# Attention, MoE and a second MoE on one core: who makes the swapped copy of v, and when in its step

## The chip, the cores and the metric

The kernel runs on one core of one Trainium2 chip. The metric is the time of one execution on the device in microseconds (us), taken as the median of several runs. The core has five engines that work through their own queues of instructions in order: PE (matmuls; the loading of its weights is listed as PEld), DVE, ACT (ScalarE), POOL (GpSimd) and SP, which here only issues loads. POOL also issues DMAs, and in the profile such a DMA takes POOL's own time while it is issued. A semaphore wait holds everything behind it in the same queue.

## The reference, cut to what matters

```python
def _attn_ref(q, k, v):                       # (8, 8, 576, 64) each, float32
    scores = scale * matmul(q_c, k_c^T)       # chunks of 64 tokens, each with itself
    attn = softmax(scores)
    out = matmul(attn, v_c)

x = attn_out as (4608 tokens, 512)
x = _moe_ref(x)      # tokens with x @ w_skip > 0 go through one of 8 experts, the argmax of x @ w_gate
return _moe2_ref(x)  # max(x@w1, x@w2, x@w3), relu, @ w_out
```

The change concerns the product `matmul(attn, v_c)` of the first line alone.

## The kernel before

The program has three phases. Phase 1 is the attention and the routing, in 36 steps `t` of 128 tokens; phase 2 runs the experts, phase 3 the second MoE. In phase 1 a step holds two chunks of 64 tokens for each of 8 heads. The tokens of a chunk lie in 64 of the 128 partitions, and a matmul of 64 rows takes weights and data from the same half. So for half of the (chunk, head) pairs the values `v` are wanted in the other half: `cross(t)` (L219 to L225) makes `vm[t]`, a copy of `v_all[t % 8]` with its halves swapped, in two copies of 64 x 260 floats, one for each half. DVE makes them for t = 0 and 1, POOL from t = 2 on. Four `vm` tiles exist at a time. The matmuls of `values(t)` (L301) read `v_all`, `vm` and the transposed exponentials `aT`.

In loop step t the code is written as follows, and for t below 34 the order on DVE, ACT and POOL is that of the code, and PE's is that of the code throughout the phase: rank of an earlier group of tiles; `send_id(t-9)`; loads of q and k; `cross(t)`; `pair_heads` (L231, on POOL: the copies `qr` and `kr`, two steps ahead of their use); `values(t-2)`; `scaled(t-2)` on DVE; the load of v for step t+6; `scores(t)` (L260) on PE and `shift(t)` (L269, L271) on DVE; `exp_transpose(t-1)` (L285 on PE, its copy `aT`, L288, on ACT); the transposes of q and k with copies `qT` and `kT` (L247, ACT); the gate's logits of tile t-3 (L344 on PE, copy `lg`, L349, on ACT); `exponentials(t)` (L278, ACT); the transpose of x of tile t-2 (L333 on PE) with the copy `xt` in `x_out` (L338, ACT); and then the routing of a group of four tiles in some of the steps (`route`, L360 to L389, on DVE; the rank matmuls L416 and L417 on PE), with the store of the group's rows (`store_x`, L492, issued by POOL). In eight of the steps a piece of the experts' weights is split too (L93 on ACT, L94 on DVE or POOL).

`send_id(t)` (L470) is an indirect DMA, issued by POOL: it scatters the 128 token numbers of a tile to the slots that the routing has given them in `ids_dram`. It is done from loop step 9 on, one in most steps, and stands directly ahead of `cross` on POOL's queue. Phase 2 reads the lists of each expert from `ids_dram`.

Waits are set by the framework from what instructions read and write. In the lists of instructions below a wait on `DMASW` followed by a lane's number is one for a DMA that POOL issued, `DMAHW` one for a load that SP issued, and `PE`, `DVE`, `Activation` and `Pool` stand for the engines; the end of such a name is the same everywhere and says nothing.

Of the kernel before, what the change touches and what calls it, by code (L numbers as in the profile page):

```python
# [29 lines left out]
NT = N // P  # L30
# [10 lines left out]
def kernel(  # L41
# [15 lines left out]
    nc = tc.nc  # L57
# [118 lines left out]
    NV = 8  # L176
    v_all = [apool.tile([P, H, D + 1], F32, name=f"v_all{i}", bufs=1) for i in range(NV)]
# [15 lines left out]
    def load_qk(u):  # L193
        if u % 5 < 3:
            qt = four_kb([P, H, 2 * D], F32, f"qt{u}", u % 5 == 2)
            kt = four_kb([P, H, 2 * D], F32, f"kt{u}", u % 5 == 2)
        else:
            both = bpool.tile([P, 2, H, 2 * D], F32, tag="b8", name=f"qkt{u}")
            qt, kt = both[:, 0], both[:, 1]
        if u * UT >= P * FULL:  # L200
            b0, nb = (u * UT - P * FULL) // TAIL, UT // TAIL
            for h in range(H):
                for dst, src in ((qt, q), (kt, k)):
                    link["load"] = nc.sync.dma_start(
                        dst[:, h, :], src[b0:b0 + nb, h, WHOLE:, :].rearrange("b (p r) d -> b p (r d)", r=2))
        for h0, h1 in [(0, 4), (4, 8)] if u == 0 else [(0, 8)] if u * UT < P * FULL else ():
            for off, b, s, n in pieces(u * UT, (u + 1) * UT):
                pr = slice(off // 2, (off + n) // 2)
                for dst, src in ((qt, q), (kt, k)):
                    link["load"] = nc.sync.dma_start(  # L210
                        dst[pr, h0:h1], src[b, h0:h1, s:s + n, :].rearrange("h (p r) d -> p h (r d)", r=2))
        units[u] = {"qt": qt, "kt": kt}

    def load_v(t):
        for off, b, s, n in pieces(t * P, (t + 1) * P):
            link["load"] = nc.sync.dma_start(
                v_all[t % NV][off:off + n, :, :D], v[b, :, s:s + n, :].rearrange("h k d -> k h d"))

    def cross(t):  # L219
        vn = v_all[t % NV].rearrange("p (h r) d -> p r h d", r=2)  # L220
        vm[t] = apool.tile([P, H // 2, D + 1], F32, tag="vm", name=f"vm{t}", bufs=4)
        eng = nc.vector if t < 2 else nc.gpsimd
        for par in range(2):
            to, of = slice(64 * par, 64 * par + 64), slice(64 - 64 * par, 128 - 64 * par)
            eng.tensor_copy(vm[t][to], vn[of, par])  # L225

    def pair_heads(u, g):
        un = units[u]
        for nm in ("q", "k"):
            r = apool.tile([P, 2, H // 2, D], F32, tag=nm + "r", name=f"{nm}r{u}_{g}", bufs=3)  # L230
            (nc.scalar.copy if u == 0 else nc.gpsimd.tensor_copy if u > 1 else nc.vector.tensor_copy)(  # L231
                r, un[nm + "t"][:, 4 * g:4 * g + 4, :].rearrange("p h (r d) -> p r h d", r=2))
            un[nm + "r", g] = r
# [60 lines left out]
    def values(t):  # L294
        u, s = divmod(t, 2)
        un = units[u]
        xp = two_banks("xp", f"xp{t}")[:, :, :4 * (D + 1)].rearrange("p r (h d) -> p r h d", h=4)
        for hp in range(4):
            for par, c2 in TILES:
                rows, cols = slice(64 * par, 64 * par + 64), slice(64 * c2, 64 * c2 + 64)  # L300
                nc.tensor.matmul(  # L301
                    xp[cols, par, hp, :], un["aT", s][rows, hp, cols], v_of(t, par, c2)[rows, hp, :],
                    start=True, stop=True)
        un["xp", s] = xp
# [31 lines left out]
    def x_out(t):  # L336
        xt[t] = apool.tile([P, KC, P], F32, tag="xt", name=f"xt{t}", bufs=2)
        nc.scalar.copy(xt[t], units["trx", t])  # L338
# [81 lines left out]
    def rank_out(g):  # L420
        T, nt = slice(0, SIZES[g]), SIZES[g]
        rs = apool.tile([P, GT, E], F32, tag="rrs", name=f"rrs_{g}", bufs=1)
        nc.vector.tensor_tensor(rs[:, T], picks["rk", g], picks[g][0][:, T], op=ALU.mult)
        picks["rs", g] = rs
# [43 lines left out]
    def send_id(t):  # L468
        g, j = PLACE[t]
        ins = nc.gpsimd.indirect_dma_start(  # L470
            out=ids_dram[:, :], out_offset=bass.IndirectOffsetOnAxis(ap=slots[g][:, j:j + 1], axis=0),
            in_=tok_i[:, t:t + 1], in_offset=None,
            bounds_check=P * SLOTS - 1, oob_is_err=False,
        )
        tc.declare_no_dep(ins.ins, group="ids", reason="no two tokens share a slot")
        tc.add_to_no_dep_group("ids", ins.ins)
        sent.append(ins.ins.name)
# [116 lines left out]
    vm, units, xt, groups, slots, picks, xgs, xT, link, put, sent = {}, {}, {}, {}, {}, {}, {}, {}, {}, {}, []  # L594
# [36 lines left out]
    def last_of(t):  # L631
        if 0 <= t < NT:
            g, j = PLACE[t]
            if j + 1 == SIZES[g]:
                return g
        return None

    for t in range(NT + LAG):
        u, s = divmod(t, 2)
        hand = t < HAND  # L640
        if t == HAND:
            by_hand.close()
        ranked = last_of(t - 5) if hand else None
        if ranked is not None:
            rank_out(ranked)
        if hand and t - LAG in late:
            send_id(t - LAG)
        if s == 0 and u + 5 < NU:
            load_qk(u + 5)
        if t < NT:  # L650
            cross(t)
        if u + 2 < NU:
            pair_heads(u + 2, s)
        if t == 8:
            nc.gpsimd.tensor_copy(tok_f, tok_i)
            nc.gpsimd.tensor_scalar_add(tok_f, tok_f, float(-N))
            nc.gpsimd.iota(col_i, pattern=[[1, P]], base=0, channel_multiplier=0)
            nc.gpsimd.tensor_copy(col_f, col_i)
        if 0 <= t - 2 < NT:
            values(t - 2)  # L660
            scaled(t - 2)
        if t >= 2 and t - 2 + NV < NT:
            load_v(t - 2 + NV)
        if t + 5 in CUTS:
            i = CUTS.index(t + 5)
            with tc.issue_after(link["load"].ins):
                raws_0[i] = load_raw(*expert_src(0, i))
        if t < NT:
            scores(t)
            shift(t)  # L670
        if 0 <= t - 1 < NT:
            exp_transpose(t - 1)
        if u + 1 < NU:
            qk_transpose(u + 1, s, "q")
        if 0 <= t - 3 < NT:
            logits(t - 3)
            logits_out(t - 3)
        if u + 1 < NU:
            qk_transpose(u + 1, s, "k")
        if t < NT:  # L680
            exponentials(t)
        if 0 <= t - 2 < NT:
            x_transpose(t - 2)
            x_out(t - 2)
        g = last_of(t - 3)
        if g is not None:
            routing[g] = route(g)
            advance(routing[g], BY if hand else 99)
        g = last_of(t - 4)
        if g is not None:  # L690
            advance(routing[g], 99)
            rank_of(g)
            if not t + 1 < HAND:
                rank_out(g)
        g = ranked if hand else last_of(t - 4)
        if g is not None:
            if g == 2:
                count_first()
            place(g)
            if g == FIRST or START[g] + SIZES[g] == DIRECT:  # L700
                for i in range(max(late[0], t - LAG + hand), START[g + 1]):
                    send_id(i)
                late = range(START[g + 1], NT - 2)
            if START[g] + SIZES[g] == DIRECT:
                load_ids(ids_0[:, 2:], ids_rows[:, 2:3])
            if g == FIRST:
                fill_first(run[(g + 1) % 2][:, 0, 0:1])
                load_ids(ids_0[:, :2], ids_rows[:, :2])
                xgs[0] = [four_kb([P, XW], F32, f"xg_0_{j}") for j in range(2)]
                rows = START[g + 1] * P  # L710
                fetch = t + 3
        if t in CUTS:
            i = CUTS.index(t)
            expert_piece(0, i, wpool, nc.gpsimd if t in ASIDE else None, raw=raws_0[i])
        if t == fetch:
            at = cpool.tile([P, 2], I32, name="at")
            nc.vector.tensor_single_scalar(at, ids_0[:, :2], rows - 1, op=ALU.min)
            for j in range(2):
                gather(xgs[0][j], at[:, j:j + 1], rows)
        if not hand and t - LAG in late:  # L720
            send_id(t - LAG)
# [411 lines left out]
    for b, (r0, n) in enumerate(BLOCKS):  # L1133
# [31 lines left out]
        for half in range(2):  # L1165
            for i in range(n // P):
# [11 lines left out]
                r = r0 + half * n + i * P  # L1178
# [34 lines left out]
```

## Time and profile before

| | us |
|---|---|
| median of 3 runs | 1156.57 |
| lowest and highest run | 1155.0, 1159.43 |
| profiled execution, its own time | 1154.31 |
| its span (first to last instruction) | 1152.6 |
| TensorE busy in the span | 1057.8 (92%) |
| ScalarE busy | 418.8 (36%) |
| GpSimd busy | 373.5 (32%) |
| exponentials of step 31 begin | 220.25 |

The last line places phase 1 in the span: its first 32 of 36 steps fill about the first fifth. The profile's times are those of the profiled execution; it lies 2.26 us below the median. The granted clock of TensorE is told as a share of its full speed: 1.00 is 2.4 GHz and 0.50 is 1.2 GHz, and the mean of a stretch lies between them.

### The profile page before, as it was taken

The page shows a single profiled execution, that of the slowest core. Times are in us where ns is not written, and L with a number is a line of the kernel's source. Part 1 is how long each engine was busy: PE and PEld are TensorE (multiplying, and loading weights), DVE is VectorE, ACT ScalarE, POOL GpSimd, SP SyncE. Part 2 cuts the span into 40 slices and gives each one's busy share as a digit, 9 for nine tenths or more (in the row PEclk, how much of TensorE's full clock was granted, in tenths as well). Part 3 has the DMA queues.
Part 4 walks back from the last instruction along what each step waited for, and adds up shares of the span by engine and source line. Part 5 has one row for each costly group of instructions (what it writes and reads, how often), then busy time and mean ns, then how long its engine had stood idle before and what let it go on. Part 6 is the DMA issues. An engine that isn't in the chain of part 4 may idle for free. (4 is left out here: it accounts for less than half of the span.)

```text
span 1152.6 us, 19706 instructions
## 1 busy us (share of the span) xinstructions
PE 1057.8 (92%) x7544; PEld 903.5 (78%) x7544; DVE 581.6 (50%) x1116; ACT 418.8 (36%) x737; POOL 373.5 (32%) x413
## 2 busy tenths in 40 slices
PE   8978777889799998899799889999999999999996
PEld 7867676878688877888678678888888888878995
DVE  4653445556685638743259793444424452443241
ACT  5553434423443424442144343232322241322231
POOL 3534535646343315442143323121401241112021
PEclk9895777769899999899999999999999999999999
DMA  9996554226676446752788864665456644666581
GB/s 233 269 275 185 140 150 123 89 76 191 247 283 211 153 142 208 257 189 94 237 260 288 282 201 156 183 192 172 156 148 191 193 137 145 192 192 200 183 275 37
DMA packets 213041, 217.13 MB, mean 188 GB/s; under 512 B 48203, under 2 KB 177227, under 8 KB 212928
## 3 DMA queue, kind: packets, MB, share of 16 engines
q1 hardware_dynamic: 199744, 174.18, 50.8%
q0 software_dynamic: 10592, 33.20, 8.3%
q10 hardware_dynamic: 2592, 8.26, 1.9%
q8 instruction: 70, 1.15, 0.4%
q14 instruction: 43, 0.35, 0.1%
HBM read 175.15 MB, written 41.83 MB: 188 GB/s over the span
## 5 line engine op out<-in xcount | busy, mean ns | idle before, releaser
L94 POOL TENSOR_TENSOR fh<-best,fh 128x512 fp32r<-128x512 f32 (+1 forms) x60 | 76.4, 1279 | 357.6 <-ACT fh L93 272.6
L768 PE MATMUL f_a<-x_t,ws 128*128 128x512 f32 (+1 forms) x270 | 101.1, 374 | 5.0 <-DVE p L1096 4.7
L769 PE MATMUL f_a<-x_t,ws 128*128 128x512 f32 (+1 forms) x270 | 100.0, 370 | 0.0
L770 PE MATMUL f_a<-x_t,ws 128*128 128x512 f32 (+1 forms) x270 | 99.8, 370 | 0.0
L93 ACT CAST whi_e<-raw_e 128x1024 fp32r<-128x1024 f32 x64 | 66.2, 1051 | 62.9 <-DMA raw_e<-in_moe_w_dram 30.3
L768 PE MATMUL h<-xhi,whi_e 128*128 128x256 f32 x256 | 75.3, 294 | 13.4 <-ACTq L1045 6.5
L769 PE MATMUL o<-wlo_m,fh 128*128 128x512 f32 x216 | 84.6, 392 | 0.0
L768 PE MATMUL o<-whi_m,fh 128*128 128x512 f32 x216 | 83.4, 392 | 0.0
L770 PE MATMUL o<-whi_m,fh 128*128 128x512 f32 x216 | 83.4, 392 | 0.0
L768 PE MATMUL y<-whi_e,hhi 128*128 128x512 f32 x184 | 74.1, 405 | 0.6 <-ACT hhi L835 0.6
L769 PE MATMUL h<-xlo,whi_e 128*128 128x256 f32 x256 | 74.2, 290 | 0.0
L94 POOL TENSOR_TENSOR wlo_e<-raw_e,whi_e 128x1024 fp32r<-128x1024 f32 x23 | 58.2, 2531 | 49.4 <-ACT whi_e L93 48.6
L770 PE MATMUL h<-xhi,wlo_e 128*128 128x256 f32 x256 | 73.8, 290 | 0.0
L770 PE MATMUL y<-whi_e,hlo 128*128 128x512 f32 x184 | 73.1, 401 | 0.3
L94 DVE TENSOR_TENSOR wlo_e<-raw_e,whi_e 128x1024 fp32r<-128x1024 f32 x41 | 53.3, 1316 | 39.4 <-ACT whi_e L93 38.3
L769 PE MATMUL y<-wlo_e,hhi 128*128 128x512 f32 x184 | 72.6, 396 | 0.0
L93 ACT CAST fh<-best 128x512 fp32r<-128x512 f32 (+1 forms) x60 | 34.7, 578 | 92.9 <-DVE best L1098 61.4
L301 PE MATMUL xp<-vm,aT 64*64 64x65 f32 x576 | 38.5, 270 | 32.4 <-POOL vm L225 31.8
L768 PEld LDWEIGHTS h<-xhi,whi_e 128*128 128x128 f32 x256 | 51.0, 199 | 16.3 <-ACTq L1045 10.0
L768 PEld LDWEIGHTS f_a<-x_t,ws 128*128 128x128 f32 x270 | 51.3, 190 | 14.7 <-DVE p L1096 5.2
L1101 ACT COPY p<-f_a 128x512 f32<-128x512 f32 (+1 forms) x45 | 24.6, 546 | 97.0 <-PE f_a L770 96.2
L759 POOL DMA_INDIRECT x_dram<-xg,ids_sb x20 | 21.3, 1066 | 116.6 <-DVEq L983 46.7
(220 smaller groups left out, 2796.1 us busy)
## 6 DMA issues: line engine op xcount, KB each, us to landing
ws<-m_sums SPq DMA_DIRECT2D x135, 512.0 KB
raw_e<-in_moe_w_dram SPq DMA_DIRECT2D x64, 512.0 KB
ws<-m_sums SPq DMA_DIRECT2D x45, 256.0 KB
x<-x_dram SPq DMA_DIRECT2D x36, 256.0 KB
x_dram<-xg POOLq DMA_DIRECT2D x8, 1040.0 KB
v_all<-in_v_dram SPq DMA_DIRECT2D x32, 256.0 KB
out_dram<-os SPq DMA_DIRECT2D x32, 256.0 KB
m_sums<-n_raw ACTq DMA_DIRECT2D x18, 448.0 KB
```

The lines of the kernel that those rows point to most:

```text
L93: nc.scalar.copy(hi, src),
L94: eng.tensor_tensor(lo, src, hi.bitcast(F32), op=ALU.subtract),
L301: nc.tensor.matmul(xp[cols, par, hp, :], un["aT", s][rows, hp, cols], v_of(t, par, c2)[rows, hp, :], start=True, stop=True)
L759: ins = nc.gpsimd.indirect_dma_start(out=x_dram[:, :], out_offset=bass.IndirectOffsetOnAxis(ap=ids, axis=0), in_=xg, in_offset=None, bound ...
L768: nc.tensor.matmul(acc, ahi, bhi, start=first, stop=False, skip_group_check=onto)
L769: nc.tensor.matmul(acc, ahi, blo, start=False, stop=False, skip_group_check=onto)
L770: return nc.tensor.matmul(acc, alo, bhi, start=False, stop=last, skip_group_check=onto)
L1101: nc.scalar.copy(p1, acc_a)
```

## The change

`cross(t)` keeps the allocation of `vm[t]` and POOL's copy into partitions 64 to 127 (from t = 2 on). The copy that reads partitions 64 to 127, and writes 0 to 63, moves to a new function `cross_up(t)`, which is called at the end of the step, behind `x_out(t-2)` and ahead of the routing; it is made by ACT from t = 2 on. For t = 0 and 1 DVE makes both copies there, where before it made them at the start of the step.

```diff
     def cross(t):
         vn = v_all[t % NV].rearrange("p (h r) d -> p r h d", r=2)
         vm[t] = apool.tile([P, H // 2, D + 1], F32, tag="vm", name=f"vm{t}", bufs=4)
-        eng = nc.vector if t < 2 else nc.gpsimd
-        for par in range(2):
-            to, of = slice(64 * par, 64 * par + 64), slice(64 - 64 * par, 128 - 64 * par)
-            eng.tensor_copy(vm[t][to], vn[of, par])
+        if t > 1:
+            nc.gpsimd.tensor_copy(vm[t][64:], vn[:64, 1])
+
+    def cross_up(t):
+        vn = v_all[t % NV].rearrange("p (h r) d -> p r h d", r=2)
+        if t < 2:
+            nc.vector.tensor_copy(vm[t][64:], vn[:64, 1])
+        (nc.vector.tensor_copy if t < 2 else nc.scalar.copy)(vm[t][:64], vn[64:, 0])
...
         if 0 <= t - 2 < NT:
             x_transpose(t - 2)
             x_out(t - 2)
+        if t < NT:
+            cross_up(t)
         g = last_of(t - 3)
```

POOL's queue around step 19 before, in the order in which it is worked off, with each instruction's waits. `xg` are the rows of a finished group, `tok_i` and `rslot` the token numbers and their slots.

```order
L316 MEMSET xg_1917 128x4x7 [waits DMASW2_49]
L492 DMA x_dram<-xg_1506 128x4x520 [waits DVE_49]
L470 DMA ids_dram<-tok_i,rslot_1795 36864x1
L225 COPY vm_2001<-v_all_133 64x260 [waits DMAHW3_49,DMASW0_49,Pool_49]
L225 COPY vm_2001<-v_all_133 64x260 [waits Pool_49]
L231 COPY qr_1_2004<-qt_1284 128x512 [waits PE_49,Pool_49]
L231 COPY kr_1_2006<-kt_1285 128x512 [waits PE_49]
```

The same place on POOL now:

```order
L320 MEMSET xg_1916 128x4x7 [waits DMASW2_49]
L496 DMA x_dram<-xg_1505 128x4x520 [waits DMASW7_49,DVE_49]
L474 DMA ids_dram<-tok_i,rslot_1795 36864x1 [waits DMASW0_49]
L223 COPY vm_2001<-v_all_133 64x260 [waits DMAHW3_49,Activation_49,Pool_49]
L235 COPY qr_1_2003<-qt_1284 128x512 [waits PE_49,Pool_49]
L235 COPY kr_1_2005<-kt_1285 128x512 [waits PE_49]
```

One of the two copies is gone, and the first one has no wait on a DMA of POOL's any more: in its place it waits for ACT (the copy into the same `vm` buffer four steps earlier). The DMAs wait for a `DMASW` lane themselves now, that of the DMA which used the lane eight of POOL's DMAs before.

ACT's queue over one step before, from one `aT` to the next:

```order
L288 COPY aT_1039<-trp_1034 128x512 [waits PE_49,Activation_49]
L247 COPY qT_943<-trq_1_1041 128x2x2x128 [waits PE_49]
L349 COPY lg_698<-lp_1047 128x9 [waits PE_49]
L247 COPY kT_956<-trk_1_1053 128x2x2x128 [waits PE_49]
L278 ACTIVATE ex_1032<-ex_1032 128x512 [waits DVE_49]
L338 COPY xt_1065<-trx_1060 128x512 [waits PE_49,Activation_49]
L288 COPY aT_1132<-trp_1127 128x512 [waits PE_49,Activation_49]
```

The same step on ACT now:

```order
L292 COPY aT_1038<-trp_1033 128x512 [waits PE_49,Activation_49]
L251 COPY qT_942<-trq_1_1040 128x2x2x128 [waits PE_49]
L353 COPY lg_697<-lp_1046 128x9 [waits PE_49]
L251 COPY kT_955<-trk_1_1052 128x2x2x128 [waits PE_49]
L282 ACTIVATE ex_1031<-ex_1031 128x512 [waits DVE_49]
L342 COPY xt_1064<-trx_1059 128x512 [waits PE_49,Activation_49]
L229 COPY vm_984<-v_all_131 64x260 [waits DMAHW4_49,Pool_49]
L292 COPY aT_1131<-trp_1126 128x512 [waits PE_49,Activation_49]
```

A copy of 64 x 260 has come in between `xt` and the next step's `aT`. It waits for the load of this step's v and for POOL's copy into the same buffer four steps earlier. The order of PE's instructions is the same through phases 1 and 2; in phase 3, where a list scheduler sets the order, matmuls of the feature products and some small work on DVE and POOL stand in another order, with the same instructions.

## Rows read from the trace of the kernel before

**Rows 1.** The page: span, busy time, PE's granted clock and the DMA share in 40 slices

```profile
span 1152.6 us, 19706 instructions
PE 1057.8 (92%) x7544; PEld 903.5 (78%) x7544; DVE 581.6 (50%) x1116; ACT 418.8 (36%) x737; POOL 373.5 (32%) x413
...
PEclk9895777769899999899999999999999999999999
DMA  9996554226676446752788864665456644666581
```

**Rows 2.** Stretches of phase 1: length, busy time of each engine, granted clock, DMA share, GB/s

```profile
core 0: us, PE busy (x) PEld busy (x) DVE busy (x) ACT busy (x) POOL busy (x), PEclk, DMA share, GB/s
21.44:37.18 15.74, 15.24 (x358) 14.37 (x354) 10.03 (x24) 11.62 (x25) 8.67 (x18) 1.00 1.11 260
41.82:68.55 26.73, 23.78 (x446) 21.64 (x446) 17.56 (x61) 14.81 (x32) 11.67 (x23) 0.87 1.09 290
45.00:51.00 6.00, 6.00 (x75) 5.67 (x77) 2.40 (x10) 2.98 (x6) 2.67 (x6) 0.50 1.17 275
54.44:68.55 14.11, 12.45 (x268) 11.16 (x264) 10.26 (x37) 8.93 (x21) 4.79 (x8) 1.00 1.10 294
68.55:220.25 151.70, 116.34 (x1682) 105.63 (x1682) 71.97 (x210) 63.05 (x127) 74.90 (x117) 0.70 0.56 156
103.33:111.91 8.58, 8.07 (x91) 7.28 (x89) 3.33 (x11) 2.97 (x8) 3.98 (x8) 0.50 0.56 142
```

**Rows 3.** Waits in 68.55 to 220.25: waiting group <- releaser, idle us, count, longest

```profile
POOL vm L225 <- issue: 72.0, 18, 6.9
...
PE xp L301 <- POOL vm L225: 31.8, 12, 5.3
...
ACT aT L288 <- PE trp L285: 70.4, 19, 7.9
```

**Rows 4.** POOL's timeline: start, us, instruction [idle before it <- releaser]

```profile
52.17 0.85 POOL L225 COPY vm<-v_all 64x260 f32<-64x260 f32 x2 [3.38 <-DMA ids_dram<-tok_i,rslot]
...
126.68 1.01 POOL L470 DMA_INDIRECT ids_dram<-tok_i,rslot  x1 [0.30 <-issue]
131.34 0.86 POOL L225 COPY vm<-v_all 64x260 f32<-64x260 f32 x2 [3.65 <-issue]
132.26 0.61 POOL L231 COPY qr<-qt 128x512 f32<-128x512 f32 x1
132.81 0.61 POOL L231 COPY kr<-kt 128x512 f32<-128x512 f32 x1
...
210.10 0.98 POOL L470 DMA_INDIRECT ids_dram<-tok_i,rslot  x1 [0.30 <-issue]
212.46 0.85 POOL L225 COPY vm<-v_all 64x260 f32<-64x260 f32 x2 [1.38 <-DMA ids_dram<-tok_i,rslot]
...
214.61 0.86 POOL L225 COPY vm<-v_all 64x260 f32<-64x260 f32 x2
```

**Rows 5.** PE's timeline, at two of the places where it stood

```profile
42.71 0.19 PE L416 MATMUL rk<-roh,upper_b 128*128 128x32 bf16 x1 [1.47 <-DVE roh L381]
...
131.79 0.82 PE L301 MATMUL xp<-vm,aT 64*64 64x65 f32 x3 [3.26 <-POOL vm L225]
```

**Rows 6.** ACT's timeline, at its copies of `aT` and exponentials

```profile
35.01 0.59 ACT L288 COPY aT<-trp 128x512 f32<-128x512 f32 x1 [0.54 <-PE trp L285]
...
41.82 0.63 ACT L278 ACTIVATE ex<-ex 128x512 f32<-128x512 f32 x1 [0.67 <-DVE ex L271]
...
54.44 0.63 ACT L278 ACTIVATE ex<-ex 128x512 f32<-128x512 f32 x1
...
56.89 0.59 ACT L288 COPY aT<-trp 128x512 f32<-128x512 f32 x1 [1.35 <-PE trp L285]
```

**Rows 7.** Groups of ACT in 68.55 to 220.25: count, busy us, mean ns, idle before

```profile
L278 ACT ACTIVATE ex<-ex 128x512 f32<-128x512 f32 x19 | 11.9, 628 | 0.0
...
L349 ACT COPY lg<-lp 128x9 f32<-128x9 f32 x19 | 3.2, 168 | 7.3 <-PE lp L344 6.6
```

**Rows 8.** The tile `vm`: duration ns min/median/max, first and last start, forms

```profile
L225 POOL COPY vm<-v_all x68: 393/400/1407, 18.8 to 240.6; 64x260 f32<-64x260 f32 x68
L225 DVE COPY vm<-v_all x4: 290/292/293, 12.2 to 14.6; 64x260 f32<-64x260 f32 x4
```

## Prediction

> **What bounds the kernel now.** I first read the page for the whole span. TensorE is busy 92% of it [rows 1], so what counts is where it stands and at which clock it runs. The clock row names the place: nearly all slices are at 9, and the low ones (8, 5, 7, 7, 7, 7) lie at the front, where the DMA row falls from 9 to 4 and 2 at the same time. That is phase 1.
>
> Next, phase 1 cut into stretches by the begins of ACT's exponentials, one per step, of which each stretch's count gives the steps [rows 2, 7]. From step 2 to step 6 (21.44 to 37.18) four steps take 15.74 us, 3.94 each, at clock 1.00. From step 9 to step 12 (54.44 to 68.55) three take 14.11, 4.70 each, at clock 1.00 and a DMA share of 1.10. From step 12 to step 31 (68.55 to 220.25) nineteen steps take 151.70, 7.98 each, with the clock at 0.70 and a DMA share of 0.56. Nothing in the code of a step grows twofold there, and the loads, which filled the DMA engines before, have room. So neither PE's work nor the loads set the pace of the long stretch.
>
> The list of waits of that stretch says what does [rows 3]. PE stands 31.8 us for POOL's `vm`, and POOL itself stands 72.0 us, 18 times, ahead of just that copy. POOL's timeline shows the place: a scatter of token numbers is issued at 126.68 and takes 1.01 us, then POOL stands 3.65 us, and only then copies `vm` [rows 4]. The profile names no releaser there ("issue"), but at 52.17 and 212.46 it names the scatter, and the list of instructions has a wait of the first copy on a DMA that POOL issued itself. At 214.61, with no scatter ahead, the copy begins at once. So one step's copy waits until the previous instruction's scatter has landed. One turn of POOL is then 1.0 for the scatter, 72.0/18 = 4.0 for the landing, 0.86 for two `vm` copies and about 1.2 for `qr` and `kr`, 7.1 in all, and now and then a store, a memset or a piece of weights: this comes to the 7.98 of a step.
>
> The price is doubled by the clock. PE stands for `vm` [rows 5], and where it has stood the next rows are at 0.50: after a stand of 1.47 us at 42.71 the stretch 45 to 51 is at 0.50 though PE is busy all 6.00 us of it, and one step at that level takes 8.58 us (103.33 to 111.91), 8.07 of them busy [rows 2]. Busy time of PE in the long stretch is therefore no measure of its work.
>
> **The change, part by part.** *POOL.* The copy that stands behind the scatter loses its wait on it. No other instruction in phase 1 takes that wait over: the scatters themselves now wait for a lane used eight POOL DMAs earlier; with five such DMAs in four steps (four scatters and a store) that is 6.4 steps, 30 us at a pace of 4.70, against a landing of 4. One copy of 0.40 us [rows 8] is gone too. A turn of POOL is then about 1.0 + 0.43 + 1.2 = 2.6 us, with a store's 0.8 and a memset every fourth step, below any pace that PE has shown. POOL stops being the bound.
>
> *What is late next.* PE and the loads. The 1.10 of the DMA share is the most that a stretch of some length shows; the long stretch moved 0.56 x 151.7 = 85 units, which at 1.10 takes 77 us, or 4.07 a step. For the pace I have three rows: 3.94 (no scatters and no full buffers yet: the gain's upper end, 151.7 - 19 x 3.94 = 76.8); 4.70 (the nearest: scatters, routing and full DMA engines, and POOL two steps ahead, so that nothing waits for it); and 5.35 = 26.73/5 for 41.82 to 68.55, which holds one fall of the clock behind a routing group (lower end: 151.7 - 19 x 5.35 = 50.0). I take 4.70, that is 89.3 us, and one such fall, 26.73 - 5 x 4.70 = 3.2. The stretch is then 92.5 us long and the gain 59.2.
>
> The Trainium skill says in "TensorE: Matmul & The Clock Gate", section "HAM oscillation — how this bites in real kernels", that a loop whose matmuls wait for a transfer in each round is set back to the lower clock round after round. The trace agrees: 0.70 over the long stretch, with twelve stands of up to 5.3 us. By its rule, too, ending the stands gives the clock back.
>
> The Trainium skill puts the fixed cost of a DMA from GpSimd at about 2.0 us ("DMA: Bandwidth & Descriptors", section "Anatomy of one DMA — SWDGE (gpsimd) path"). The 4.0 us here, behind the 1.0 of the issue, are twice that. By the page's figure the wait removed would be 19 x 2.0 = 38 us and the time some 1119; I go by the rows.
>
> *ACT.* It gains 34 copies of 64 x 260. There is no such copy on ACT; 9 columns take 0.168 and 512 columns 0.586 to 0.63 [rows 6, 7], so about 0.40 for 260 by interpolation, 13.6 us in all. In the long stretch ACT stands 70.4 us ahead of `aT` [rows 3], just where the copy comes in, and at the faster pace still about 1.35 a step [rows 6]: it is hidden. In the dense early steps the gap is 0.54 at 35.01, so a copy of 0.40 fits by little. Bounds for steps 2 to 11: 0, and 10 x 0.40 = 4.0 if none is hidden. I take +1.0. If the cover went altogether, 13.6 us would be lost. The wait on v's load is covered too: at 52.17 POOL's copy for step 9 is released by the scatter and not by the load, and ACT's comes behind the exponentials at 54.44.
>
> *Steps 0 and 1 on DVE.* Two copies of 0.29 [rows 8] go behind `shift`, whose results are wanted first. Between 0 and -0.6; I take 0.
>
> *Phases 2 and 3.* PE's order in phase 2 is the same; phase 3's new order has the same instructions. I take 0 and put up to 6 us either way into the range, about half a per cent, as no row shows it.
>
> *Sum*, against the profiled execution: 1154.31 - 59.2 + 1.0 = 1096.1. The median of the runs lies 2.26 above it: 1098.4, rounded to 1098.
>
> **Rivals.** *Only the waits go.* PE's 31.8 us vanish, but its clock stays at the present mean, because small stands such as the routing's [rows 5] hold it down: 1156.57 - 31.8 = 1124.8. For it: 42.71 shows that 1.47 us were enough there. Against it: 54.44 to 68.55 contains routing and scatters and is at 1.00.
>
> *The change doesn't free POOL.* If the 4 us were POOL's own preparation of the scatter and not the wait, they would move to the next instruction, and only 19 x 0.43 = 8 us of copy go: 1148. Against it: the four scatters that end at 210.10 follow each other closely, and the copy at 212.46 stands only 1.38 us behind the last of them.
>
> *Gain given back downstream.* Phase 2 could be tied to something that phase 1 doesn't move, its expert weights above all, and the end would stay at 1157. Against it: the DMA engines have over 60 us of free share in phase 1, and the weights' loads follow those of v on the same queue, so they come earlier too.
>
> *Slower: ACT's copy holds up PE.* On ACT the copy waits for v(t), two steps before PE needs it, ahead of `aT`. If loads came later than `aT` is due, all of ACT's later copies would stand behind it and PE would stand each step as at 42.71, staying at the lower clock all the way. From step 7 on, 24 steps of 8.58 would then end at 41.82 + 206 = 248 instead of 220.25: 1156.6 + 27.5 = 1184. It decides once the copy is later than the gap of 0.54 to 1.35 us by a microsecond in most steps. For it: the DMA engines are full in this pace. Against it: the load of step 9 was there 2 us ahead of the place of the new copy.
>
> **How the numbers follow.** My forecast, POOL freed and the clock with it, has 0.78: between 1156.6 - 76.8 = 1079.8 and 1156.6 - 50.0 + 4.0 = 1110.6, likeliest 1098. Only the waits: 0.10 (1125). Not freed: 0.04 (1148, still 0.7% faster). Given back: 0.03. ACT in the way: 0.05 (1184). The range is 1079 to 1126: the forecast with its bounds and the first rival, 0.88 of the cases by themselves and some 0.8 with phase 3's uncertainty. A measurement can tell about 0.5% from no change; faster by more than that 0.92, within it 0.03, slower 0.05.
>
> **What would show it.** In the profile of the changed kernel the row of POOL's `vm` waiting for "issue" or for the scatter should be gone and POOL's copies run within a microsecond of the scatter before; PE's wait on `vm` should be near nothing; the clock should be close to 1.00 in 60 to 160 us, with a DMA share of 0.9 or more; the exponentials of step 31 should begin at 160 to 165 instead of 220.25; ACT's new copy should take about 0.4 us and `aT` wait less for `trp`. I would be wrong if the copy on ACT is seen waiting for a load, if PE waits for `aT` or for routing in most steps with the clock at 0.50, or if the rest of the span, from the end of phase 1 on, grows by what phase 1 loses.

## The result and the profile after

The changed kernel takes 1126.22 us (median of 4 runs, 1119.18 to 1127.98) against 1155.78 of the kernel before in the same comparison (1153.82 to 1159.43). The ratio is 0.973 with a 95% interval of 0.968 to 0.978: faster by 2.7%. Forecast were 1098 us and 5.1%. The direction and the place are right, about half of the size came, and the measured median lies 0.2 us above the stated range. The ratios here and below, unlike the medians, leave out runs well above the fastest of their version: one each of the added transposes (1101.87, the profiled one), of all subtractions on POOL (1116.3) and of the second combination (1263.17, whose trace is therefore not used).

The page of the kernel after, to be read against [rows 1]. The profiled execution took 1125.63 us.

```profile
span 1123.9 us, 19739 instructions
PE 1035.0 (92%) x7544; PEld 881.6 (78%) x7544; DVE 577.0 (51%) x1116; ACT 432.9 (39%) x771; POOL 356.4 (32%) x379
...
PEclk9898888698999998999999999999999999999998
DMA  9999572246783737471998924664466545666681
```

The low clock at the front is shorter than before, but not gone: 8, 8, 8, 8, 6. Next the stretches; the columns are those of [rows 2], and the first row holds steps 2 to 6, as 21.44 to 37.18 did before. The second runs from the exponentials of step 12 to those of step 31, as 68.55 to 220.25 did before.

```profile
20.10:38.83 18.73, 16.94 (x368) 15.91 (x364) 10.08 (x24) 13.67 (x30) 7.05 (x14) 0.91 1.03 246
71.37:189.21 117.84, 95.42 (x1678) 85.75 (x1668) 68.95 (x202) 71.43 (x146) 57.21 (x88) 0.84 0.71 192
119.15:143.22 24.07, 19.97 (x374) 18.12 (x374) 14.62 (x43) 14.66 (x31) 12.36 (x20) 0.86 0.51 153
130.00:134.00 4.00, 4.00 (x77) 3.77 (x76) 2.67 (x12) 2.64 (x6) 0.65 (x1) 0.59 0.30 85
138.00:141.00 3.00, 3.00 (x67) 2.88 (x61) 2.11 (x5) 0.34 (x1) 1.87 (x4) 0.51 0.30 97
```

The nineteen steps take 117.84 us instead of 151.70. Where the time went: step 12 is reached 2.8 us later than before (71.37 against 68.55), the nineteen steps save 33.9, the four steps from 31 to 35 take 2.2 longer (their exponentials begin at 189.21 and 213.03, against 220.25 and 241.92), and what follows step 35 is as long as before to 0.2 us. That makes 28.7, the difference of the spans. Hardly anything was given back later; nearly all of the missing half is missing in the nineteen steps: forecast were 92.5 us for them, 25.3 less than they took.

The waits of that stretch in the kernel after (columns as in [rows 3]) are other ones:

```profile
POOL x_dram L496 <- DVE sm L322: 41.2, 5, 9.0
ACT aT L292 <- PE trp L289: 19.6, 8, 6.0
DVE wlo_e L94 <- ACT whi_e L93: 19.5, 5, 5.7
...
PE trx L337 <- DVE xg L324: 9.8, 8, 2.0
...
PE rk L421 <- DVE run L389: 4.7, 4, 1.2
...
PE rk L420 <- DVE roh L385: 3.7, 4, 1.1
```

POOL's 72.0 us ahead of `vm` are gone, and so are PE's 31.8 for it. POOL now waits for DVE, as an engine with time to spare. PE waits for DVE instead: for the scaled rows `xg`, which is new, and, in four groups of four tiles, twice for the routing's results, 8.4 us where it was 2.3 before.

POOL's timeline shows the step that the change was about, to be held against 126.68 to 132.81 in [rows 4]:

```profile
119.63 0.99 POOL L474 DMA_INDIRECT ids_dram<-tok_i,rslot  x1 [0.16 <-issue]
120.66 0.39 POOL L223 COPY vm<-v_all 64x260 f32<-64x260 f32 x1
121.12 0.61 POOL L235 COPY qr<-qt 128x512 f32<-128x512 f32 x1
121.67 0.61 POOL L235 COPY kr<-kt 128x512 f32<-128x512 f32 x1
```

The copy begins 0.04 us after the scatter has been issued. The turn takes 2.65 us; 2.6 were forecast.

PE's stands in the four steps from 119 to 143, and then what DVE and ACT did ahead of the first of them:

```profile
129.41 0.63 PE L337 MATMUL trx<-ident,xg 128*128 128x128 f32 x4 [1.96 <-DVE xg L324]
136.04 0.19 PE L420 MATMUL rk<-roh,upper_b 128*128 128x32 bf16 x1 [0.37 <-DVE roh L385]
137.42 0.18 PE L421 MATMUL rk<-run,ones_b 128*128 128x32 bf16 x1 [1.19 <-DVE run L389]
```

```profile
126.95 1.22 DVE L94 TENSOR_TENSOR wlo_e<-raw_e,whi_e 128x1024 fp32r<-128x1024 f32 x1 [3.48 <-ACT whi_e L93]
128.09 0.16 DVE L322 TENSOR_SCALAR sm<-xp 128x8 f32<-128x8 f32 x1
```

```profile
125.43 0.41 ACT L229 COPY vm<-v_all 64x260 f32<-64x260 f32 x1
125.87 1.04 ACT L93 CAST whi_e<-raw_e 128x1024 fp32r<-128x1024 f32 x1
```

DVE stands 3.48 us in its queue for the cast of a piece of the experts' weights, and behind that stands the scaling that PE wants: PE stands 1.96. In the rows of stretches, the clock is 0.59 from 130 to 134, after this stand, and 0.51 from 138 to 141, after those of the routing, with PE busy throughout both. So the stands are one part of the price and the low clock behind them another. The runs below take the two apart.

### The profile page after: what moved, and what is told of

Same layout as the page of the kernel before. It is cut to its first block, busy times and chain, and to the rows that moved or that the text cites. A ratio compares the mean times of both kernels' runs of the same rounds, so it can differ in the third digit from the quotient of the medians.

```text
span 1123.9 us, 19739 instructions
## 1 busy us (share of the span) xinstructions
PE 1035.0 (92%) x7544; PEld 881.6 (78%) x7544; DVE 577.0 (51%) x1116; ACT 432.9 (39%) x771; POOL 356.4 (32%) x379
## 4 chain that ended last, share of the span: by engine, by line
PE 42%; DMA 5%; issue 3%; POOL 1%; DVE 1%; SPq 0%; ACT 0%; POOLq 0%; DVEq 0%; ACTq 0%
PE f_a L774 5%; PE f_a L775 5%; PE f_a L776 5%; PE o L774 4%; PE o L775 4%; PE o L776 4%; DMA ws<-m_sums 3%; PE f_d L774 3%; PE f_d L776 3%; PE f_d L775 3%; DMA m_sums<-n_q 1%; PE f_b L774 1%; PE f_b L776 1%; PE f_b L775 1%; PE trf L948 1%
## 5 line engine op out<-in xcount | busy, mean ns | idle before, releaser
L775 PE MATMUL y<-wlo_e,hhi 128*128 128x512 f32 x184 | 72.5, 396 | 0.0
L94 DVE TENSOR_TENSOR wlo_e<-raw_e,whi_e 128x1024 fp32r<-128x1024 f32 x41 | 50.8, 1256 | 35.9 <-ACT whi_e L93 34.0
L774 PEld LDWEIGHTS f_a<-x_t,ws 128*128 128x128 f32 x270 | 51.1, 189 | 10.1 <-DVE best L1102 1.5
L776 PEld LDWEIGHTS f_a<-x_t,ws 128*128 128x128 f32 x270 | 51.1, 189 | 8.6
L775 PEld LDWEIGHTS f_a<-x_t,ws 128*128 128x128 f32 x270 | 51.1, 189 | 8.4
```

What stands on the lines that cost most here:

```text
L94: eng.tensor_tensor(lo, src, hi.bitcast(F32), op=ALU.subtract),
L774: nc.tensor.matmul(acc, ahi, bhi, start=first, stop=False, skip_group_check=onto)
L775: nc.tensor.matmul(acc, ahi, blo, start=False, stop=False, skip_group_check=onto)
L776: return nc.tensor.matmul(acc, alo, bhi, start=False, stop=last, skip_group_check=onto)
```

## Experiments

**Which half POOL copies.**

```diff
-            nc.gpsimd.tensor_copy(vm[t][64:], vn[:64, 1])
+            nc.gpsimd.tensor_copy(vm[t][:64], vn[64:, 0])
...
-            nc.vector.tensor_copy(vm[t][64:], vn[:64, 1])
-        (nc.vector.tensor_copy if t < 2 else nc.scalar.copy)(vm[t][:64], vn[64:, 0])
+            nc.vector.tensor_copy(vm[t][:64], vn[64:, 0])
+        (nc.vector.tensor_copy if t < 2 else nc.scalar.copy)(vm[t][64:], vn[:64, 1])
```

> The changed kernel with the two halves exchanged: POOL, at the start of the step, makes the copy that reads partitions 64 to 127 and ACT, at the end, the one that reads 0 to 63. Number, size, engine and place of all copies are those of the changed kernel; in the list of instructions only POOL's wait on its own scatter is back. Theory (the landing of the scatter on POOL's queue was the whole pace): POOL's row of standing ahead of vm is back at about 4 us a step, only one copy of 0.4 us less a turn than before, 19 x 0.43 = 8 us, so about 1148 (0.993 of before). Rival (what counted is that POOL makes one copy less and ACT takes it): as the changed kernel, 1126 (0.974).

Measured: 1139.33, 0.990 of before (0.986 to 0.994). The waits of its nineteen steps:

```profile
PE xp L305 <- POOL vm L223: 30.4, 15, 5.4
POOL vm L223 <- DMA ids_dram<-tok_i,rslot: 27.6, 7, 5.6
...
POOL vm L223 <- issue: 19.9, 5, 5.8
POOL vm L223 <- ACT vm L229: 10.1, 2, 6.2
```

POOL stands ahead of `vm` once in each of the nineteen steps again, 74.5 us in all and 3.9 in the mean, as the 4.0 before. The profile names the scatter for 27.6 us of it, nothing for 19.9, and instructions of ACT for 27.0 (10.1 of them in the last row); the changed kernel's copy waits for ACT as well and does not stand there, so ACT is hardly the reason. PE stands 30.4 us for `vm`, as in [rows 3], and the greater part of the gain is gone, though ACT relieves POOL of just as many copies. The greater part of the gain is the wait on the scatter's landing and not the work moved off POOL; the 1.0% that stays is about the 0.7% of one copy less in a turn. In the lists of instructions this wait stands at a copy of POOL's that reads partitions 64 to 127, and at none that reads 0 to 63; why the framework sets it there stays open.

**POOL makes the late copy.**

```diff
-        (nc.vector.tensor_copy if t < 2 else nc.scalar.copy)(vm[t][:64], vn[64:, 0])
+        (nc.vector.tensor_copy if t < 2 else nc.gpsimd.tensor_copy)(vm[t][:64], vn[64:, 0])
```

> The changed kernel with the copy at the end of the step made by POOL instead of ACT (DVE for steps 0 and 1, as there). POOL then waits for its scatter at the end of its turn, behind qr and kr. Theory: what counts is that the copy is not late for PE; a turn of POOL is 1.0 + 4.0 + 0.4 = 5.4 us with the wait running beside vm, qr and kr, below the 5.95 a step that the changed kernel takes in steps 12 to 28, so about the changed kernel's time, 1120 to 1132 (0.97 to 0.98). Rival (POOL must not wait at all, and ACT's help is needed): POOL stands ahead of the late copy and PE again for vm, 1140 or more (0.987).

Measured: 1125.12, 0.979 of before (0.973 to 0.986). The theory's range is met; whether ACT is better by a few tenths of a per cent (0.973 there) can't be told. The waits show that POOL still stands, but later in its turn; the second view is its stretch from step 12 to step 31:

```profile
POOL vm L229 <- DMA ids_dram<-tok_i,rslot: 46.5, 17, 5.4
...
PE xp L305 <- POOL vm L229: 19.5, 10, 3.5
```

```profile
66.41:193.96 127.55, 101.50 (x1682) 92.42 (x1681) 68.95 (x202) 63.53 (x127) 73.42 (x113) 0.79 0.72 190
```

What helped was to take `qr`, `kr` and one copy out from behind the landing, and in the whole time that is had without ACT. Not all of PE's wait goes in this version: 19.5 us. The stretch is 9.7 us longer than with ACT's copy; in these two profiled executions that is made up outside it (step 12 comes 5.0 us earlier, steps 31 to 35 take 2.7 less, and what follows 4.7 less). So 24 of the 34 us that the nineteen steps save are had by the later place, and the rest there goes with ACT's help.

**The rank matmuls one step later.**

```diff
-        if ranked is not None:
-            rank_out(ranked)
...
             shift(t)
+        if ranked is not None:
+            rank_of(ranked)
+            rank_out(ranked)
...
-            rank_of(g)
             if not t + 1 < HAND:
+                rank_of(g)
                 rank_out(g)
```

> The changed kernel with the two rank matmuls of a group of tiles and the product on DVE that reads them moved from the end of a step into the next one, behind its scores and shift. Theory (what took half of the expected gain are PE's stands behind the routing, and the lower clock after them): PE's waits of 8.4 us on the routing's results go in steps 12 to 31, and of the time at 0.50 behind them about as much again, so 1110 (0.960). Rival (the stands only move to the next wait in the step, or the expert weights' split on DVE sets the pace): 1124 to 1128 (0.973).

Measured: 1121.54, 0.974 (0.968 to 0.980): the rival's number, no difference from the changed kernel that can be told. The waits of its nineteen steps, and the stretch itself, show why:

```profile
PE trx L337 <- DVE xg L324: 12.6, 9, 2.4
...
PE lp L348 <- DVE rrs L427: 7.5, 4, 1.9
...
PE rk L421 <- DVE run L389: 4.3, 4, 1.1
```

```profile
72.49:185.74 113.25, 88.89 (x1683) 79.22 (x1682) 70.53 (x210) 70.60 (x146) 58.27 (x88) 0.89 0.76 205
```

The stand for `roh` is gone, that for `run` is as long as before, and a new one of 7.5 us has come in, since the logits' matmuls need the PSUM bank (a part of the memory that matmuls write to) that DVE is still reading the ranks from. The stands were moved, not removed: PE stands 24.4 us in this stretch (113.25 - 88.89), against 22.4 in the changed kernel. What the rank's place is worth by itself is not told by this.

**PE kept busy where it stood, in the changed kernel.**

```diff
         tr = ps_tr(f"trx{t}").rearrange("p (c t) -> p c t", c=KC)
+        for _ in range(6 if 8 < t < HAND - 4 and t % 4 in (0, 1) else 0):
+            nc.tensor.transpose(tr[:, 0, :], ident, ident)
...
-        rk = ps_sm(f"rk{g}")[:, :nt * E].rearrange("p (t e) -> p t e", e=E)
+        bank = ps_sm(f"rk{g}")
+        for _ in range(14 if START[g] + nt < HAND - 4 else 0):
+            nc.tensor.transpose(bank[:, P:2 * P], ident, ident)
+        rk = bank[:, :nt * E].rearrange("p (t e) -> p t e", e=E)
```

> The changed kernel with work added on PE and nothing taken away: 14 transposes of the identity, whose result nobody reads, ahead of each group's rank matmuls, and 6 ahead of the transpose of x in the steps around a routing, so that PE is busy where it stood. Theory (the lower clock after the stands, not the stands themselves, costs the larger part): the granted clock in steps 12 to 28 rises from 0.87 to 0.95 or more and the time falls by 8 to 17 us in spite of the added work, 1109 to 1118 (0.960 to 0.967). Rival (the chain over DVE and ACT sets the pace, PE's clock doesn't matter): no change or slower by the added work, 1126 to 1140.

Measured: 1092.62 (1085.09 to 1101.87), 0.948 of before (0.941 to 0.955). That is more than the theory asked for, with work added and none taken away. The stretch from step 12 to step 31, and the two groups of added transposes in it (PE; busy us, mean ns, idle before):

```profile
68.11:168.29 100.18, 91.10 (x1802) 83.19 (x1792) 69.19 (x202) 71.18 (x146) 60.09 (x89) 1.00 0.87 230
```

```profile
L337 PE MATMUL trx<-ident 128*128 128x128 f32 x60 | 8.3, 274 | 0.0
L423 PE MATMUL rk<-ident 128*128 128x128 f32 x64 | 7.8, 272 | 0.0
```

The clock is 1.00 over all nineteen steps, and they take 100.18 us instead of 117.84. From these rows PE's own work at full clock can be estimated: 91.10 less 16.1 of added transposes is 75.0, or 3.95 a step, close to the 3.94 that steps 2 to 6 of [rows 2] take. With this estimate the other rows can be split. Before, of 151.70 us, 75.0 are work, 41.3 the lower clock (116.34 - 75.0) and 35.4 PE standing. After, 75.0 are work, 20.4 the lower clock and 22.4 standing. The change took away 13.0 of standing and 20.9 of low clock.

**PE kept busy where it stood, in the kernel before.**

```diff
-        xp = two_banks("xp", f"xp{t}")[:, :, :4 * (D + 1)].rearrange("p r (h d) -> p r h d", h=4)
+        banks_xp = two_banks("xp", f"xp{t}")
+        for _ in range(16 if 8 < t < HAND - 4 else 0):
+            nc.tensor.transpose(banks_xp[:, 0, 384:], ident, ident)
+        xp = banks_xp[:, :, :4 * (D + 1)].rearrange("p r (h d) -> p r h d", h=4)
```

> The kernel before with work added on PE and nothing taken away: 16 transposes of the identity, whose result nobody reads, ahead of the value matmuls in each of the steps 9 to 29, where PE stood for vm. Theory (before the change POOL's turn with the landing in it, 7.1 to 8.0 us, is the pace by itself, and PE's lower clock only came with it): POOL's standing ahead of vm stays at about 4 us a step and the time falls by no more than the 17 us between 19 x 7.98 and 19 x 7.1, 1138 to 1156 (0.985 to 1.0). Rival (the clock is the larger part before the change as well): the time falls by 30 us or more, to the changed kernel's 1126 (0.974) or below.

Measured: 1151.21, 0.995 of before (0.992 to 0.998). Its stretch from step 12 to step 31, and two rows of its waits there:

```profile
69.33:220.06 150.73, 131.26 (x1985) 122.67 (x1984) 71.20 (x210) 62.72 (x127) 72.76 (x117) 0.88 0.58 157
```

```profile
POOL vm L225 <- issue: 74.0, 18, 6.2
...
PE xp L304 <- POOL vm L225: 15.2, 9, 3.6
```

The same means does next to nothing here: the clock rises from 0.70 to 0.88, PE's wait is halved, and the nineteen steps take 150.73 us against 151.70. POOL stands 74.0. So before the change POOL's turn was the pace by itself, and the low clock cost next to nothing of its own; after the change the clock does.

**All subtractions of the first expert's weights on POOL.**

```diff
     CUTS = [13, 17, 19, 21, 25, 27, 29, 33]
-    ASIDE = (19, 27)
+    ASIDE = CUTS
```

> The changed kernel with the subtraction of all eight pieces of the first expert's weights on POOL instead of two there and six on DVE. Theory (DVE's wait for ACT's cast, 19.5 us in five of the steps 12 to 31, is what holds up scaled and then the transpose of x on PE, and starts the lower clock there): PE's waits of 2 us for xg go in four steps, with about as much for the clock behind them, so 1110 to 1118 (0.960 to 0.967). Rival (POOL's turn with 2.4 us more makes vm late, or the routing alone starts the lower clock): 1124 to 1130 (0.972 to 0.977).

Measured: 1108.11 (1098.13 to 1116.3), 0.955 of before (0.947 to 0.963); the median lies below the theory's range, the interval reaches into it. Two rows of its waits and its stretch from step 12 to 31:

```profile
POOL wlo_e L94 <- ACT whi_e L93: 28.1, 5, 7.6
...
PE trx L337 <- DVE xg L324: 1.7, 3, 0.6
```

```profile
71.00:179.23 108.23, 96.92 (x1683) 86.94 (x1682) 66.12 (x197) 71.12 (x145) 67.68 (x91) 0.80 0.79 209
```

The wait for ACT's cast now lies on POOL, where it holds nobody up. PE's stands fall from 22.4 to 11.3 us (108.23 - 96.92), and the nineteen steps by 9.6. The second half of the theory is wrong: the low clock costs as much as in the changed kernel (96.92 - 75.0 = 21.9). What holds it down was not tested apart: the stands for the routing are left (3.6 us for `roh`, 1.6 for `run`), and so is a long step from 28 to 29 (11.17 us), of which more below.

**ACT's copy behind the routing's exponential.**

```diff
             x_out(t - 2)
-        if t < NT:
-            cross_up(t)
...
             expert_piece(0, i, wpool, nc.gpsimd if t in ASIDE else None, raw=raws_0[i])
+        if t < NT:
+            cross_up(t)
```

> The changed kernel with ACT's copy of v moved from behind xt to the end of the step's code, behind the routing's exponential and the cast of the expert weights, ahead of the next aT. Theory (the copy's 0.41 us stands in the chain of the routing, in which DVE waits 1.1 us for the exponential in each group, and in that of the cast): 0.41 us less in ten places and part of the lower clock behind them, 2 to 8 us, 1118 to 1124 (0.967 to 0.972). Rival (hidden there as forecast): 1125 to 1128 (0.973 to 0.975).

Measured: 1122.21, 0.972 (0.964 to 0.979). It doesn't tell the two apart: both numbers lie in the interval. One row of its waits and its stretch from step 12 to 31:

```profile
PE trx L337 <- DVE xg L324: 4.8, 4, 1.4
```

```profile
69.57:186.57 117.00, 98.19 (x1678) 88.38 (x1668) 73.10 (x202) 70.58 (x146) 57.42 (x88) 0.81 0.74 198
```

PE's stand for `xg` is halved (4.8 us against 9.8), so the copy was a part of it, but the nineteen steps are only 0.8 us shorter.

**Combinations.** The first has the added transposes, all subtractions on POOL and ACT's late copy; the second the subtractions on POOL and of the transposes only those ahead of the rank; the third all transposes and the late copy. Their edits are those above.

> The changed kernel with the transposes of the identity of e7_filler, all subtractions of the first expert's weights on POOL, and ACT's copy of v at the end of the step's code. If the three act apart, the time is below that of the added transposes alone: 1085 to 1092 (0.940 to 0.947). If the added transposes already take away what the other two would save, it is the same as theirs, 0.948.

> The changed kernel with all subtractions of the first expert's weights on POOL, and of the transposes of the identity only the 14 ahead of each group's rank matmuls. Theory (in e10_combined the 6 transposes ahead of the transpose of x stood where PE no longer waits, and cost what they take): 0.85 us a group less than there for six groups and the clock still near 1.00, 1085 to 1095 (0.940 to 0.949). Rival (the 2.4 us on POOL make qr late and PE falls to the lower clock there): as e10_combined, 0.956.

> The changed kernel with the transposes of the identity of e7_filler and ACT's copy of v at the end of the step's code, the subtractions where the changed kernel has them. Theory (with the clock held, ACT's copy is hidden where the change puts it): as e7_filler, 0.945 to 0.951. Rival (0.41 us in the routing's chain in each group shows once the clock no longer covers it): 2 to 4 us less, 0.944 or below.

Measured: 1104.63, 0.956 (0.950 to 0.963); 1094.75, 0.947 (0.943 to 0.951); 1092.14, 0.948 (0.944 to 0.951). Two means that each save something are no better together, and the first combination is probably worse than the transposes alone (0.948; the intervals overlap). The first one's stretch from step 12 to 31, and in it the step from 29 to 30:

```profile
67.81:172.00 104.19, 95.81 (x1792) 88.84 (x1781) 67.55 (x201) 71.30 (x146) 70.40 (x94) 0.95 0.89 232
156.24:165.62 9.38, 7.00 (x61) 6.65 (x61) 3.10 (x9) 4.55 (x8) 7.33 (x10) 0.63 1.05 225
```

Its clock is 0.95. The second combination, without the six transposes ahead of `x`, is at 0.947, as its theory said: they would be plain work where the subtractions on POOL have already removed PE's stand. But the late copy is also missing in it, and the first one's trace points elsewhere. Its step from 29 to 30 takes 9.38 us at a clock of 0.63, where the same step of the group before takes 4.10 (25 to 26); these 5.3 us are more than the 4.0 by which its stretch is longer than that of the transposes alone. So what makes the first combination worse stays open.

In the third, ACT's place makes no difference that can be told (0.948 with it as without). Two rows of its waits from step 12 to 31 show a new one:

```profile
PE trx L337 <- ACT aT L292: 5.4, 1, 5.4
ACT whi_e L93 <- DMA raw_e<-in_moe_w_dram: 5.3, 1, 5.3
```

Here too the step from 29 to 30 is long, 11.17 us: ACT stands 5.3 us for the load of a piece of the experts' weights, and its copy of v and `aT` stand behind that, so that PE stands as well. At this pace a load has come to set the time in one place.

The best versions run are thus the changed kernel with added transposes, at 0.947 to 0.948 of before, which is 2.6% below the changed kernel.

## Why the prediction was half right

**What bounds the kernel** was right: POOL's turn with the scatter's landing in it. The exchanged halves show that the wait is the greater part of it (0.990), and the kernel before with PE kept busy shows that neither PE nor its clock was (0.995).

**POOL's turn** after the change: 2.65 us measured, 2.6 forecast. No other instruction took the wait over.

**ACT's copy** takes 0.41 us where 0.40 was estimated, and in the nineteen steps ACT has room for it, but for the 0.8 us that its later place takes off them. Step 12 came 2.8 us later than before instead of the 1.0 taken, inside the bounds of 0 and 4. The loss lies in steps 2 to 6, the first row of stretches above: 18.73 us at a clock of 0.91, against 15.74 at 1.00. Whether ACT's copy is the cause stays open: where POOL makes the late copy they took 17.1, and the versions with the same copy in the same place as far as step 7 reached step 12 between 67.8 and 72.5. One stand of PE's, 1.8 us at 26.59 ahead of the transposes of the exponentials, may belong to it: the list of waits names no releaser for it, the view of the copy's line counts it among those who waited for the copy. ACT's wait for v's load, the rival that ended slower, was not seen: the new copy stood once in the whole run, for 1.1 us at 197.33, where no engine or load is named, and the clock rose.

**The step that failed** is "what is late next", in the choice of the row for the pace and in "one such fall". 4.70 us a step came from 54.44 to 68.55, and the nineteen steps took 6.20 each, above even the 5.35 that was set as the bound. So the time lies outside the case that was given 0.78, which ended at 1110.6. Three things were overlooked.

- The stretch that served as a witness holds no piece of the experts' weights; the first comes in step 13. In the long stretch there are seven, and DVE stands up to 5.7 us for ACT's cast in five of them, with the scaled rows behind that. The row was in the trace of before as well, but there POOL's wait covered it (23.4 us in five stands, the first row below). The subtractions on POOL show its size: 9.6 us in the nineteen steps, and step 35 begins 12.8 us earlier; in all it is 0.973 to 0.955, and what is more than that in the whole time has no place found for it.
- The clock fell many times instead of once, behind PE's stands for `xg` and for the routing. The term was 3.2 us, and the lower clock took an estimated 20.4 after the change. PE stands up to 1.1 and 1.2 us for the rank in each of four groups, together more than the 1.47 of [rows 5] that should have been the warning. In the witness PE has stood for a routing too, 0.9 and 0.4 us, without a fall; why that one did not start it was not settled.
- One step alone, from 28 to 29, took 11.46 us, where it took 3.99 with the added transposes. That is 7.5 of the 25.3 us by which the nineteen steps missed the forecast, in part stands and lower clock that the estimate above holds already. PE stands in it among the scores' matmuls with no releaser shown (the last section has more); its cause stays open.

DVE's wait in the kernel before, from 68.55 to 220.25, and the long step in the kernel after:

```profile
DVE wlo_e L94 <- ACT whi_e L93: 23.4, 5, 5.3
```

```profile
166.55:178.01 11.46, 8.72 (x91) 7.46 (x89) 2.98 (x9) 3.52 (x8) 7.05 (x11) 0.65 0.20 53
```

**The signs** named in advance came where they spoke of POOL, of PE's wait for `vm` and of ACT (`aT` waits 19.6 us for `trp` instead of 70.4). The clock was to be close to 1.00 and is 0.84 over the nineteen steps, the DMA share was to be 0.9 and is 0.71, and step 31 was to come at 160 to 165 and came at 189.21.

**The rivals.** In number the first rival came out, 1124.8 for "only the waits go", and the reason given for it, small stands like the routing's, is what the trace shows. Its mechanism is not quite that: the clock did rise, from 0.70 to 0.84, and PE's wait of 31.8 us was not simply gone, as new stands brought it from 35.4 to 22.4 in all. That its number fits is chance: what came is 13.0 us of stands and 20.9 of clock, less the 5.2 lost outside the nineteen steps. The rivals "not freed" and "given back downstream" fall with POOL's timeline and with the time from step 35 on, which is the same to 0.2 us (in the profiled executions of the other versions it lies between 899 and 916, so such an equality is good to a few microseconds only).

**The range** ended at that rival's number and was too narrow above by the unknown next bound: with the main case's upper end taken from a stretch that lacked part of the work, 1126 was no bound.

**The Trainium skill's rule on the clock** ("TensorE: Matmul & The Clock Gate", section "HAM oscillation — how this bites in real kernels") bears on the half that failed as well: the stands need not be for a DMA. Here the waits for DVE, of 1 to 2 us, set the clock back round after round, as the rows at 0.59 and 0.51 and the clock of 1.00 with PE kept busy show. The Trainium skill's 2.0 us for a DMA from GpSimd ("DMA: Bandwidth & Descriptors", section "Anatomy of one DMA — SWDGE (gpsimd) path") would have given 1119, seven below the measured time; but the wait itself was 4.0 and did go in full, so that the nearness says nothing for the figure. That is luck.

## What to carry to other kernels

When a wait that bounds a stretch goes, the next bound is found in the waits that it covered, so read those of the same stretch (here DVE's for the cast, and PE's for the routing) rather than the pace of a neighbouring stretch that lacks part of the work. On PE stands of a microsecond or two can cost about as much again at the lower clock (here 22.4 and 20.4 us); to learn which of the two counts, keep PE busy with work that nobody reads and look at whether the time falls. A wait on one's own DMA is worth looking for in the list of instructions: the same copy of the other half had none, though why was not found.

## What the runs showed of the hardware

- With 14 transposes of 128 x 128 added ahead of each group's rank and 6 ahead of the transposes of `x` in two of four steps, PE's granted clock was 1.00 over the nineteen steps (100 us), in which it had been 0.84, and the kernel became 2.6% faster (0.973 to 0.948).
- ACT's copy of 64 x 260 floats across partitions takes 410 ns, POOL's 390 to 400 and DVE's 292.
- In the changed kernel's profile PE stood five times between 168.3 and 172.5 us (around step 28), 0.2 to 1.3 us each and 2.7 in all, for which no releaser is shown, and step 29 began 11.5 us after step 28. The late copy and all subtractions on POOL show the same there (11.15 and 11.17 us), the first combination one step later (9.38). The added transposes alone do not. What PE waited for stays open.
